# Values loaded by batch, ten weight units beside the packing, and products of another form, in a fused attention and expert kernel

## The chip, the cores and the metric

The kernel runs on one core of a Trainium2 chip. The metric is the device time of one execution in microseconds, the median of several runs, against the kernel before. The core has TensorE (PE, the matrix engine), VectorE (DVE), ScalarE (ACT), GpSimd (POOL) and SyncE (SP, which only issues transfers here), each with its own queue of instructions, taken in order. An instruction waits at the head of its queue until what it reads has been written and what it overwrites is free, and everything behind it waits too.

## The reference

Three parts follow each other. A packed attention with 8 batches (B), 8 heads (H), 576 positions (S), 64 dimensions a head and 32 pack rows: the pack rows attend to the keys and values, then every query attends to the packed rows. Its output, 4608 tokens of 512 values, goes through a feed-forward layer with 2048 hidden values, and the result through a layer with 8 experts, of which each token takes the one with the largest gate value.

```python
p_packed = sm_attn(p, k, v)                 # 32 packed rows per head
x = sm_attn(q, p_packed, p_packed)          # then [4608, 512]
h = x @ w_in                                # 512 -> 2048
g = np.where(h >= 1, h, np.where(h <= -1, 0.0, (h + 1) ** 2 / 4))
x = g @ w_out                               # 2048 -> 512
e = argmax(x @ w_gate)                      # one of 8 experts per token
out = softmax(x @ w_gate)[e] * (np.maximum(x @ w1[e], 0) @ w2[e])
```

## The kernel before

**Numbers in two parts.** Weights and activations of the large products are split into a high and a low part of a narrower type (F32R). A product of two such numbers is three matmuls: high by high, high by low, low by high.

**The packing** (function packing, loop over i from 0 to 17, NG = 16 iterations with work). Iteration i is one half of the heads of one batch. It has these steps: the keys are loaded into one of three buffers kp (L371), the values into one of three buffers vr (L379, L380; rows of 256 floats, 1 KB); PE makes the scores sc (L388); DVE takes the largest of each row, nm (L395), and scales it (L396); ACT takes the exponent (L398), with the sums rs, which DVE inverts (L399, L400); PE transposes the exponents in tp and av (L406, L408); ACT copies them into tA and tB, which lie behind the values in the buffer vr (L409 to L411); one iteration later PE multiplies them with the values (av, L421), and ACT scales the result into packed (L422).

**Weight units.** The first feed-forward layer has its weights in 16 units (FC) of 1 MB, as 64-bit numbers. Unit u is loaded by load_unit (L275) into a raw buffer of the list RAW and split by prep_unit: ACT Abs (L290), DVE L291 to L294 on 1024 elements a partition, ACT cast (L295), DVE subtraction (L296). Of four units the first two are input weights (ws), the other two output weights (wo). NU = 12 units are prepared in the packing, evenly over its 16 iterations, each two loads ahead; units 12 to 15 are prepared by late_unit in steps 3 to 6 of the first tile.

**Products.** The second attention is folded into the first layer: for a pair of batches p and each n from 0 to 3, the packed rows pk are multiplied with the input weights ws into pw (buffers pw0n and pw1n). For the first pair, first_product makes them from the units in place: for (n, g) and each of two halves par, 6 matmuls of 128x512 (L323), one cast on ACT (L326) and one subtraction on DVE (L327), each on 128 partitions. n = 0 and 1 are made in the packing loop, n = 2 and 3 behind it. The input weights are also spilled to memory (L299), and for later pairs reloaded and multiplied by product: for (n, k) 3 matmuls (L336), whose result is evacuated in two halves of 64 partitions (L340, L341).

**Steps.** Tile t of 12, step fc of 16: ffn1 makes h (L714: the product weights pw with the second attention's probabilities ah and al, which tile_chains makes in pieces from the queries, qr at L212), hidden makes the activation in rt (ACT L731 and L732, DVE L733) and its parts gh (ACT L747) and gl (DVE L748), two buffers of each of the three; tile_y of the step before adds into four rows of y (L719, L720, L721). The first LEAD = 3 steps are issued in the last iterations of the packing loop. The expert part begins when all tiles are done, and the change doesn't touch it.

**What sets the order.** Only SP's queue is in the order of the code. The instructions of the other engines are ordered by the framework's scheduler, by its own estimate of when each can run. Buffers are taken by tag: a tile of a tag with two buffers waits until the reader of the one before the last is done.

## Time and profile before

| | |
|---|---|
| median of 3 runs | 1271.33 us (1271.19 to 1272.02) |
| the profiled execution | 1273.13 us, its span 1271.4 us |
| mean granted TensorE clock in it | 0.981 |
| PE busy | 1205.7 us, 95% of the span |
| DVE busy | 943.2 us, 74% |
| ACT busy | 752.5 us, 59% |
| POOL busy | 420.8 us, 33% |
| moved by DMA | 128.25 MB, mean 101 GB/s |

The shares are means over stages with different limits. The change lies in the first 170 us, and there a table by stretches tells more: for each stretch it has the busy time of every engine, the granted clock, the mean share of time in which the 16 DMA engines were busy (somewhat over 1 where their packets overlap) and what they moved. A timeline gives the start of each instruction, its duration, engine, line and operation, and in brackets how long the engine had been idle and what released it. The durations of neighbours overlap, as the engines are pipelined: what an instruction costs its engine in a full queue is the distance between two starts.

### The profile page before, as it was taken

The page shows a single profiled execution, that of the slowest core. Times are in us where ns is not written, and L with a number is a line of the kernel's source. Part 1 is how long each engine was busy: PE and PEld are TensorE (multiplying, and loading weights), DVE is VectorE, ACT ScalarE, POOL GpSimd, SP SyncE. Part 2 cuts the span into 40 slices and gives each one's busy share as a digit, 9 for nine tenths or more (in the row PEclk, how much of TensorE's full clock was granted, in tenths as well). Part 3 has the DMA queues.
Part 4 walks back from the last instruction along what each step waited for, and adds up shares of the span by engine and source line. Part 5 has one row for each costly group of instructions (what it writes and reads, how often), then busy time and mean ns, then how long its engine had stood idle before and what let it go on. Part 6 is the DMA issues. An engine that isn't in the chain of part 4 may idle for free. (4 is left out here: it accounts for less than half of the span.)

```text
span 1271.4 us, 21999 instructions
## 1 busy us (share of the span) xinstructions
PE 1205.7 (95%) x7234; PEld 999.5 (79%) x7234; DVE 943.2 (74%) x2360; ACT 752.5 (59%) x1702; POOL 420.8 (33%) x682
## 2 busy tenths in 40 slices
PE   5788999999999999999999998988999999999997
PEld 3446887788778887778888876876999999989996
DVE  7787858988877859968679598698566666666663
ACT  4656646667656566566565555643656566565653
POOL 3120116624731116731112266776312112121110
PEclk8988999999999999999999999999999999999999
DMA  9994870143111232112331105201611212112150
GB/s 341 374 337 146 314 203 22 44 164 133 55 35 48 93 108 76 59 34 67 110 102 37 36 17 174 44 1 58 195 39 42 59 34 67 34 42 59 34 175 21
DMA packets 70186, 128.25 MB, mean 101 GB/s; under 512 B 10281, under 2 KB 46633, under 8 KB 66864
## 3 DMA queue, kind: packets, MB, share of 16 engines
q1 hardware_dynamic: 56464, 97.33, 23.7%
q0 software_dynamic: 5840, 18.95, 3.9%
q10 hardware_dynamic: 7760, 10.49, 2.7%
q8 instruction: 60, 0.98, 0.3%
q14 instruction: 62, 0.51, 0.1%
HBM read 162.31 MB, written 31.77 MB: 153 GB/s over the span
## 5 line engine op out<-in xcount | busy, mean ns | idle before, releaser
L714 PE MATMUL h<-ah,pw 128*128 128x256 f32 (+1 forms) x1024 | 244.0, 302 | 11.3 <-DVE rt L733 10.8
L886 PEld LDWEIGHTS gh<-gx,sw 128*128 128x128 f32 x1728 | 230.4, 192 | 14.5
L522 DVE CUSTOM_DVE_ANT_0 jk<-yr,wgb 128x512 bf16<-128x512 f32 x288 | 232.8, 808 | 5.1 <-ACT yr L773 3.2
L886 PE MATMUL gh<-gx,sw 128*128 128x256 f32 x1728 | 234.0, 284 | 0.0
L719 PE MATMUL y<-wo,gh 128*128 128x512 f32 x576 | 230.4, 400 | 1.1 <-ACT kp L398 0.6
L720 PE MATMUL y<-wo,gh 128*128 128x512 f32 x576 | 227.8, 396 | 0.0
L870 DVE TENSOR_TENSOR sw<-raw,sw 128x512 fp32r<-128x512 f32 x264 | 169.4, 692 | 76.3 <-ACT sw L869 76.3
L714 PEld LDWEIGHTS h<-ah,pw 128*128 128x128 f32 x1024 | 176.7, 190 | 36.5 <-DVE rt L733 20.3
L869 ACT CAST sw<-raw 128x512 fp32r<-128x512 f32 x304 | 169.3, 617 | 60.7 <-PE gy L721 54.2
L721 PE MATMUL y<-wo,gl 128*128 128x512 f32 x576 | 191.8, 399 | 2.4 <-POOL gl L748 2.0
L731 ACT ACTIVATE rt<-h,half 128x320 f32<-128x320 f32 (+1 forms) x192 | 110.9, 580 | 111.1 <-PE h L714 74.9
L714 PE MATMUL h<-al,pw 128*128 128x256 f32 (+1 forms) x512 | 152.6, 298 | 0.3 <-POOL al L243 0.3
L747 ACT CAST gh<-rt 128x256 fp32r<-128x256 f32 (+2 forms) x256 | 100.6, 417 | 86.8 <-DVE rt L733 64.6
L733 DVE SCALAR_TENSOR_TENSOR rt<-h,rt 128x320 f32<-128x320 f32 (+1 forms) x192 | 105.4, 550 | 62.0 <-ACT rt L732 60.3
L721 PEld LDWEIGHTS y<-wo,gl 128*128 128x128 f32 x576 | 106.0, 188 | 30.8 <-POOL gl L748 5.4
L719 PEld LDWEIGHTS y<-wo,gh 128*128 128x128 f32 x576 | 108.6, 188 | 25.0 <-issue 2.1
L720 PEld LDWEIGHTS y<-wo,gh 128*128 128x128 f32 x576 | 108.9, 189 | 18.4
L854 POOL TENSOR_TENSOR gx<-xT,gx 128x1024 fp32r<-128x1024 f32 (+1 forms) x19 | 45.1, 2373 | 235.9 <-ACT gx L853 220.8
L719 PE MATMUL gy<-sw,ggh 128*128 128x512 f32 x288 | 114.5, 398 | 0.0
L720 PE MATMUL gy<-sw,ggh 128*128 128x512 f32 x288 | 114.4, 397 | 0.0
L890 ACT ACTIVATE ggh<-gh 128x256 fp32r<-128x256 f32 x144 | 54.9, 382 | 98.5 <-PE gh L886 94.2
L748 DVE TENSOR_TENSOR gl<-rt,gh 128x64 fp32r<-128x64 f32 (+1 forms) x192 | 92.9, 499 | 22.7 <-ACT gh L747 15.9
(222 smaller groups left out, 1859.7 us busy)
## 6 DMA issues: line engine op xcount, KB each, us to landing
raw<-in_w2cat SPq DMA_DIRECT2D x76, 1024.0 KB
ws<-wsd SPq DMA_DIRECT2D x48, 512.0 KB
wr<-in_wcat SPq DMA_DIRECT2D x16, 1024.0 KB
kp<-in_kT SPq DMA_DIRECT2D x16, 576.0 KB
xb<-xs SPq DMA_DIRECT2D x72, 128.0 KB
vr<-in_vv SPq DMA_DIRECT2D x16, 512.0 KB
wsd<-ws SPq DMA_DIRECT2D x8, 1024.0 KB
qr<-in_qT ACTq DMA_DIRECT2D x16, 320.0 KB
```

The costliest lines, as they stand in the source:

```text
L522: dve.tensor_tensor_reduce(out=junk, in0=rows[j][:, :DM], in1=wgb[0][:, e, :], scale=1.0, scalar=0.0, op0=ALU.mult, op1=ALU.add, accum_out ...
L714: pe.matmul(ps[:, col0:col0 + n], lhsT=w[:, g, part, c], rhs=x[:, g, col0:col0 + n], start=(n_mm == 0), stop=(n_mm == 5))
L719: pe.matmul(y, lhsT=gh, rhs=wh, start=first, stop=False)
L720: pe.matmul(y, lhsT=gh, rhs=wl, start=False, stop=False)
L721: pe.matmul(y, lhsT=gl, rhs=wh, start=False, stop=last)
L731: act.activation(v[:, :W], ps[:, :W], AF.Relu, bias=half, scale=0.5)
L733: dve.scalar_tensor_tensor(out=v[:, :W], in0=ps[:, :W], scalar=1.0, in1=v[:, :W], op0=ALU.max, op1=ALU.min)
L747: act.copy(hi, v[:, c0:c1])
L748: lo_eng.tensor_tensor(out=lo, in0=v[:, c0:c1], in1=f32(hi), op=ALU.subtract)
L869: act.copy(w[:, 0, :], r)
L870: lo_engine(sid, i, n).tensor_tensor(out=w[:, 1, :], in0=r, in1=f32(w[:, 0, :]), op=ALU.subtract)
L886: pe.matmul(ps[:, :SL], lhsT=first(sid, 4 * (fc // 4) + k, part)[:, c], rhs=rh[:, k, :], start=(n_mm == 0), stop=(n_mm == 3 * KD - 1))
```

## The change

The loads of the values: s1_load_v now takes a batch at a time. 512 of its 576 rows go into one buffer as four consecutive rows of 512 floats for each partition (8 KB in one piece), the other 64 into a work tile (named vq) of tag rt. To fit, the transposes of iteration i take every fourth column of the exponents. tA and tB become work tiles of the tags gh and gl, and the third buffer of the values, wo6, becomes a fourth buffer for raw units, which are loaded three ahead.

The units: 10 instead of 12 are spread over the 16 iterations, units 10 and 11 go with the two iterations behind (i = 16 and 17), units 12 to 15 stay late. The load of the last unit is issued one iteration later, and so are the loads of qr for the first tile.

The products: for n = 2 and 3, first_product uses product_of, the body of product with the weights in place.

```diff
...
-    RAW = ["wo4", "wo5", "wr"] * 4 + ["pw03", "pw13", "wo7", "wr"]
+    RAW = ["wo4", "wo5", "wr", "wo6"] * 2 + ["wo4", "wo5", "wr", "wo6", "pw03", "pw13", "wo7", "wr"]
...
         if g == 0:
             products(0, n)
+        if n > 1:
+            for q in range(2):
+                product_of(0, n, 2 * g + q, wstage[2 * n + g][:, q])
+            return
         for par in range(2):
...
         if k == 0:
             products(p, n)
+        product_of(p, n, k, ws1[0][:, k % 2])
+
+    def product_of(p, n, k, w):
         g, q = divmod(k, 2)
         ps = a_tile([P, 512], f"pp{p}_{n}_{k}")
         for i, (t, m) in enumerate(((0, 0), (0, 1), (1, 0))):
-            pe.matmul(ps, lhsT=both(k, t), rhs=ws1[0][:, q, m, :], start=(i == 0), stop=(i == 2))
+            pe.matmul(ps, lhsT=both(k, t), rhs=w[:, m, :], start=(i == 0), stop=(i == 2))
         for par in range(2):
...
-            def s1_load_v(i):
-                b, g = divmod(i, 2)
-                s = d[i]
-                va = wtile(("pw02", "pw12", "wo6")[i % 3], [P, 1280 + 640], F32, f"vr{i}")
-                s["vr"] = va[:, :1280].rearrange("p (c d) -> p c d", c=5)
-                s["tA"], s["tB"] = va[:, 1280:1280 + 384], va[:, 1280 + 384:]
-                sp.dma_start(s["vr"][:, :4, :], vv[b, :512, 256 * g:256 * g + 256].rearrange("(c p) d -> p c d", p=P))
-                sp.dma_start(s["vr"][:64, 4, :], vv[b, 512:, 256 * g:256 * g + 256])
+            vrs = {}
+
+            def s1_load_v(b):
+
+                vr = wtile(("pw02", "pw12")[b % 2], [P, 4, 512], F32, f"vr{b}")
+                rest = work.tile([P, 512], F32, name=f"vq{b}", tag="rt", bufs=2)
+                sp.dma_start(vr, vv[b, :512].rearrange("(p c) d -> p c d", c=4))
+                sp.dma_start(rest[:64], vv[b, 512:])
+                vrs[b] = vr, rest
...
-                    pe.transpose(ps[:, c * P:(c + 1) * P], s["a1"][:, c * P:(c + 1) * P], ident)
+                    pe.transpose(ps[:, c * P:(c + 1) * P], s["a1"][:, :4 * P].rearrange("p (j c) -> p c j", c=4)[:, c], ident)
...
+                s["tA"] = work.tile([P, 384], F32, name=f"tA{i}", tag="gh", bufs=2)
+                s["tB"] = work.tile([P, 256], F32, name=f"tB{i}", tag="gl", bufs=2)
...
             s1_load_v(0)
             s1_load(1)
             load_unit(1)
+            s1_load(2)
             s1_load_v(1)
-            s1_load(2)
             load_unit(2)
+            load_unit(3)
...
-                soon(3 + 2 * c, load)
+                soon(4 + 2 * c, load)
...
-                if i + 2 < NG:
-                    s1_load_v(i + 2)
-                for u in range(-(-NU * i // NG), min(-(-NU * (i + 1) // NG), NU)):
+                if 2 <= i < NG - 2 and i % 2 == 0:
+                    s1_load_v(i // 2 + 1)
+
+                us = range(-(-(NU - 2) * i // NG), -(-(NU - 2) * (i + 1) // NG)) if i < NG else (NU - 2 + i - NG,)
+                for u in us:
                     prep_unit(u)
-                    if 0 < u < NU - 2:
-                        load_unit(u + 2)
+                    if 0 < u < NU - 3:
+                        load_unit(u + 3)
...
                 if i == NG - 1:
-                    for u in range(NU, FC):
+                    for u in range(NU, FC - 1):
                         load_unit(u)
+                if i == NG:
+                    load_unit(FC - 1)
...
```

From L318 on the lines move down by some: the score is now L396, nm L403 and L404, the value product L432, h L730, y L735 to L737, rt L749, gh L763 and gl L764, and the halves of a product L347 (ACT) and L348 (DVE).

Where instructions moved, the orders of the two programs show it. PE's queue at the end of the packing, of before; sc_1186 and sc_1238 are the scores of iterations 14 and 15, av_1166 the value product of 13, y_2 the first row of y, tp_1219 the transposes of 14:

```order
L388 MATMUL sc_1186<-kp_164 64x288 x4
L719 MATMUL y_2_1362<-wo_356,gh_1306 128x512
L720 MATMUL y_2_1362<-wo_356,gh_1306 128x512
L421 MATMUL av_1166<-vr_1059 32x64 x20
L388 MATMUL sc_1238<-kp_160 64x288 x4
L721 MATMUL y_2_1362<-wo_356,gl_1307 128x512
L714 MATMUL h_2_1383<-ah_193,pw_0_0_592 128x256
...
L406 MATMUL tp_1219<-ident,kp_164 128x128 x4
```

And of after, from the last transpose of iteration 14 (av_1218); av_1276 is the value product of 15, pp_2_0 the first product of n = 2:

```order
L416 MATMUL av_1218<-ident,kp_164 64x128
L396 MATMUL sc_1234<-kp_160 64x288 x4
L730 MATMUL h_1_1346<-ah_197,pw_0_0_585 128x256
...
L432 MATMUL av_1218<-vr_1117,tA_1220 32x64 x12
L432 MATMUL av_1218<-vr_1117,tB_1221 32x64 x4
L432 MATMUL av_1218<-vq_1118,tB_1221 32x64 x4
L416 MATMUL av_1276<-ident,kp_160 64x128
L414 MATMUL tp_1271<-ident,kp_160 128x128 x4
L432 MATMUL av_1276<-vr_1117,tA_1278 32x64 x12
...
L343 MATMUL pp_2_0_1440<-ws_1121,pk 128x512 x3
L735 MATMUL y_0_1367<-wo_424,gh_1302 128x512
```

Before, y of step 0 is begun ahead of the score of 15; now the first y stands behind the last value product and the first product.

DVE's queue around the last two nm, of before; ca_1178 is unit 10, rt_1308 and rt_1354 are the hidden steps 0 and 1:

```order
L733 SCALAR_TENSOR_TENSOR rt_1308<-h_0_1293,rt_1308 128x512
...
L294 SCALAR_TENSOR_TENSOR ca_1178<-wr_1001,ca_1178 128x1024
L733 SCALAR_TENSOR_TENSOR rt_1354<-h_1_1339,rt_1354 128x512
L395 TENSOR_REDUCE nm_1191<-sc_1186 128x1
L296 TENSOR_TENSOR wo_1177<-ca_1178,wo_1177 128x2x512
L396 TENSOR_SCALAR nm_1191<-nm_1191 128x1
L748 TENSOR_TENSOR gl_1353<-rt_1354,gh_1352 128x512
L395 TENSOR_REDUCE nm_1243<-sc_1238 128x1
L399 TENSOR_SCALAR rs_1194<-rs_1194 128x1
```

And of after, where ca_1336 is unit 10 and nm_1239 the nm of iteration 15:

```order
L291 TENSOR_SCALAR ca_1336<-ca_1336 128x1024
L292 TENSOR_SCALAR ca_1336<-ca_1336 128x1024
L293 SCALAR_TENSOR_TENSOR ca_1336<-wr_1061,ca_1336 128x1024
L749 SCALAR_TENSOR_TENSOR rt_1304<-h_0_1289,rt_1304 128x512
L403 TENSOR_REDUCE nm_1239<-sc_1234 128x1
L294 SCALAR_TENSOR_TENSOR ca_1336<-wr_1061,ca_1336 128x1024
L404 TENSOR_SCALAR nm_1239<-nm_1239 128x1
L296 TENSOR_TENSOR wo_1335<-ca_1336,wo_1335 128x2x512
...
L764 TENSOR_TENSOR gl_1303<-rt_1304,gh_1302 128x512
```

Before, hidden steps 0 and 1 (gl_1353 closes one of them) lie among the last nm, and unit 10 is finished ahead of the last; now only the first part of hidden step 0 does, and the end of unit 10 and gl of step 0 lie behind.

DVE's queue in steps 3 to 7, of before; ca_1625 is unit 14:

```order
L291 TENSOR_SCALAR ca_1625<-ca_1625 128x1024
L748 TENSOR_TENSOR gl_1647<-rt_1648,gh_1646 128x512
L292 TENSOR_SCALAR ca_1625<-ca_1625 128x1024
L327 TENSOR_TENSOR pw_2_1_1423<-pp_2_1_1_1452,pw_2_1_1423 128x512
L293 SCALAR_TENSOR_TENSOR ca_1625<-wr_1289,ca_1625 128x1024
L296 TENSOR_TENSOR ws_1561<-ca_1562,ws_1561 128x2x512
L327 TENSOR_TENSOR pw_3_0_1504<-pp_3_0_0_1506,pw_3_0_1504 128x512
L294 SCALAR_TENSOR_TENSOR ca_1625<-wr_1289,ca_1625 128x1024
L733 SCALAR_TENSOR_TENSOR rt_1690<-h_7_1675,rt_1690 128x512
```

And of after, where ca_1508 and ca_1572 are units 12 and 13:

```order
L294 SCALAR_TENSOR_TENSOR ca_1508<-wr_1283,ca_1508 128x1024
L234 TENSOR_SCALAR sm_0_0_1433<-sm_0_0_1433 128x10
L292 TENSOR_SCALAR ca_1572<-ca_1572 128x1024
L749 SCALAR_TENSOR_TENSOR rt_1489<-h_3_1474,rt_1489 128x512
L348 TENSOR_TENSOR pw_2_1_1439<-pp_2_2_1457,pw_2_1_1439 64x512
L348 TENSOR_TENSOR pw_2_0_1438<-pp_2_3_1465,pw_2_0_1438 64x512
L235 RECIPROCAL sm_0_0_1433<-sm_0_0_1433 128x10
L293 SCALAR_TENSOR_TENSOR ca_1572<-wr_1285,ca_1572 128x1024
L296 TENSOR_TENSOR ws_1507<-ca_1508,ws_1507 128x2x512
L764 TENSOR_TENSOR gl_1488<-rt_1489,gh_1487 128x512
L348 TENSOR_TENSOR pw_2_1_1439<-pp_2_3_1465,pw_2_1_1439 64x512
```

One subtraction of 128x512 between two operations of a unit became two of 64x512, and the hidden steps stand further apart in operations.

## Rows read from the trace of the kernel before

**Rows 1.** Stretches: length, busy PE, PEld, DVE, ACT, POOL, clock, DMA share, GB/s

```profile
0.00:110.00 110.00, 78.45 (x815) 45.71 (x815) 86.17 (x169) 64.97 (x159) 26.37 (x110) 0.84 0.98 346
113.60:159.70 46.10, 45.54 (x317) 37.59 (x316) 36.62 (x56) 29.74 (x50) 3.44 (x3) 1.00 0.59 223
140.00:150.00 10.00, 10.00 (x57) 8.62 (x57) 9.47 (x16) 7.62 (x12) 2.97 (x3) 1.00 0.69 288
150.00:160.00 10.00, 10.00 (x55) 8.54 (x54) 10.00 (x13) 6.72 (x10) 0.00 (x0) 1.00 0.83 302
170.00:180.00 10.00, 10.00 (x56) 8.45 (x55) 6.40 (x12) 6.98 (x13) 2.68 (x4) 1.00 0.99 353
```

**Rows 2.** PE's timeline: start, duration (us), engine, line, operation, out<-in, shape, count

```profile
117.09 0.39 PE L719 MATMUL y<-wo,gh 128*128 128x512 f32 x1
...
117.56 0.40 PE L721 MATMUL y<-wo,gl 128*128 128x512 f32 x1
...
121.64 0.39 PE L714 MATMUL h<-ah,pw 128*128 128x256 f32 x1
...
123.17 0.39 PE L719 MATMUL y<-wo,gh 128*128 128x512 f32 x1
...
125.73 0.60 PE L406 MATMUL tp<-ident,kp 128*128 128x128 f32 x4
...
129.80 0.90 PE L421 MATMUL av<-vr 128*32 128x64 f32 x40
130.63 1.66 PE L323 MATMUL pp<-ws,pk 128*128 128x512 f32 x6
...
164.46 0.39 PE L719 MATMUL y<-wo,gh 128*128 128x512 f32 x1
```

**Rows 3.** ACT's timeline, same columns, idle time before in brackets

```profile
115.41 0.74 ACT L398 ACTIVATE kp<-sc,nm 128x576 f32<-128x576 f32 x1
...
116.80 0.64 ACT L732 ACTIVATE rt<-rt 128x512 f32<-128x512 f32 x1
...
119.47 1.05 ACT L295 CAST wo<-ca 128x1024 fp32r<-128x1024 f32 x1 [0.38 <-DVE ca L294]
...
161.89 0.62 ACT L747 CAST gh<-rt 128x512 fp32r<-128x512 f32 x1
```

**Rows 4.** DVE's timeline, same columns

```profile
113.56 0.75 DVE L395 TENSOR_REDUCE nm<-sc 128x1 f32<-128x576 f32 x1
...
152.07 0.68 DVE L327 TENSOR_TENSOR pw<-pp,pw 128x512 fp32r<-128x512 f32 x1
152.68 1.21 DVE L294 SCALAR_TENSOR_TENSOR ca<-wr,ca 128x1024 int32<-128x1024 int32 x1
153.81 0.68 DVE L733 SCALAR_TENSOR_TENSOR rt<-h,rt 128x512 f32<-128x512 f32 x1
...
159.68 0.68 DVE L733 SCALAR_TENSOR_TENSOR rt<-h,rt 128x512 f32<-128x512 f32 x1
...
169.04 0.47 DVE L226 TENSOR_REDUCE mx<-qr 128x10 f32<-128x320 f32 x1
```

**Rows 5.** Line L341: duration min/median/max in ns; who waited for it

```profile
L341 DVE TENSOR_TENSOR pw<-pp,pw x96: 645/686/696, 246.3 to 684.6; 64x512 fp32r<-64x512 f32 x96
...
  ACT pw L340: 18.4, 23
```

**Rows 6.** Waits, 0 to 110 us: us in total, times, longest

```profile
SPq L212 <- POOL al L243: 10.4, 1, 10.4
...
PE tp L406 <- ACT kp L398: 11.8, 6, 3.1
...
DVE ca L291 <- ACT ca L290: 6.0, 7, 1.3
```

**Rows 7.** Stretches with a mix of loads, and with 8 KB pieces alone

```profile
12.00:62.00 50.00, 38.17 (x432) 21.44 (x430) 42.09 (x87) 32.74 (x95) 6.45 (x19) 0.90 1.05 375
130.00:136.00 6.00, 6.00 (x70) 4.47 (x60) 4.25 (x7) 4.53 (x7) 0.00 (x0) 1.00 1.02 427
```

More of the change, by code (lines that the diff above doesn't have):

```diff
@@ L415, in s1_av @@
                 ps = s["ps"][:, :D]
+                vr, rest = vrs[i // 2]
                 for c in range(5):
@@ L420, in s1_av @@
                         r = slice(NP * j, NP * j + NP)
-                        pe.matmul(ps[r, :], lhsT=t[:, r], rhs=s["vr"][:w, c, D * j:D * j + D], start=(c == 0), stop=(c == 4))
+                        pe.matmul(ps[r, :], lhsT=t[:, r], rhs=(vr[:, c] if c < 4 else rest[:w])[:, 256 * (i % 2) + D * j:256 * (i % 2) + D * j + D], start=(c == 0), stop=(c == 4))
                 act.activation(packed[:, i, :], ps, AF.Copy, scale=s["rs"])
```

## Prediction

> **What bounds the kernel now.** I read the table of stretches first [rows 1]. In the first 110 us no engine is full: PE is busy 78.45 us, VectorE (DVE) 86.17, and the DMA engines stand at a share of 0.98. Behind that PE is the bound: 45.54 of the 46.1 us from 113.6 on, and 10.00 of 10 in the stretches that follow. So the end of the kernel moves with two things: PE work that disappears where PE is full, and the moment from which PE is fed without gaps. The packing (score, softmax, transposes and value products of iterations 0 to 15) ends late there: the last nm is taken at 113.56, the last av runs at 129.80, and the first product of the late kind (L323) at 130.63, with steps of tile 0 woven in between [rows 2, 4]. While PE is full, DVE has 46.1 - 36.62 = 9.5 us of slack between 113.6 and 159.7, but none from 150 to 160 [rows 1]. That is where this change can go either way.
>
> The profiled execution took 1273.13 us (its span 1271.4), 1.8 above the median of 1271.33. My sum is a shift against the trace of that execution, and I add it to the median.
>
> **Fewer products.** The products n=2 and n=3 take 3 matmuls of 128x512 for each of 8 k instead of 6 for each of 8 halves: 24 fewer. Two starts of such matmuls that have one between them are 0.47 us apart (117.09, 117.56) [rows 2], 0.235 each. All of them lie behind 130 us, where PE is full: 24 x 0.235 = **5.6 us less on PE**.
>
> **What that costs elsewhere.** Each such result is now evacuated in two halves of 64 partitions: 16 casts on ACT and 16 subtractions on DVE instead of 8 and 8. The later pairs already do this: 64x512 takes 686 ns [rows 5], and the 128x512 form at 152.07 took 0.68 us [rows 4]. Half the partitions are no cheaper, so 8 more are a real load. Back to back a 512-element operation holds DVE for 0.61 us (152.07 to 152.68) and a 1024-element operation of a weight unit for 1.13 (152.68 to 153.81) [rows 4].
>
> **The shared buffers.** tA, tB and the rest of V now lie in the buffers of gh, gl and rt, two of each. The order of PE shows the effect: before, y of step 0 begins ahead of sc15; now the first y stands behind av15 and a product. Up to 130.63 the kernel before had done 44 matmuls of y (10.3 us at 0.235) and the steps h_2 to h_4, each 12 matmuls of 256 columns in 1.4 to 1.5 us (121.64 to 123.17), 4.4 us [rows 2]. So 14.7 us of PE work are pushed behind av15. If PE ran without a gap from av15 on, the change would come out even with av15 ending at 130.6 - 14.7 + 5.6 = **121.5**.
>
> When does av15 end? By the order, DVE has up to nm15 two gl and one rt less (3 x 0.61), L294 and L296 of one unit less (2 x 1.13), and one pair of rs more (0.3): 3.8 us less. With idle time as before, nm15 comes at 113.56 - 3.8 = 109.8. From there: nm (0.75), the L294 that now stands behind it, and L404, together 1.9; exp and the three copies, one after the other as at 115.41 to 116.80, 1.4; the transposes 0.6; av 0.9 [rows 2, 3]. That is 4.8 if ACT is free; with the Abs and the cast of a unit ahead of these steps (1.05 as at 119.47, twice) and 0.5 for hand-overs 7.4. I take 7.4: av15 ends at 117.2. By PE alone the change would gain 121.5 - 117.2 = **4.3 us**.
>
> **Two units moved behind.** Ten units are spread over the 16 iterations, the next two go into the two iterations behind them, four stay late. I count DVE's queue up to the hidden step of h_8 (before: L733 at 159.68 [rows 4]), since by then nearly all of it is done. After has, up to there, 9 more subtractions of products (9 x 0.61 = 5.5 us), L294 and L296 of the last unit (2.3), and 3 transposes, 4 reductions and two small ones of tile chains, 0.47 or less each (as at 169.04; 3.1): **10.9 us more**. Its slack was 9.5. With a long queue DVE was idle 0.53 us in 140 to 150 and 0.00 in 150 to 160 [rows 1]; at the first rate 46 us keep 2.4, at the second none. I take 2.0, so 7.5 of slack are used and L749 of h_8 starts at 159.7 + 10.9 - 7.5 = 163.1.
>
> When must it? The y of step 8 began at 164.46 [rows 2]. After has one score of a tile chain more ahead of it (estimate 0.3, two matmuls), and like before no product behind it: the even point is 164.8. From the start of L733 to the end of its gh cast it takes 1.3 us if nothing stands ahead (0.68 and 0.62), and it took 2.83 at 159.68 to 162.51 [rows 3, 4]. With 2.0 the even point for L749 is 162.8. So DVE and not PE decides: 163.1 is 0.3 late, and **the 4.3 us that PE had gained are waited away** in steps 1 to 8. Behind them DVE is light (6.40 of 10 in 170 to 180 [rows 1]), but PE is full and gives nothing back.
>
> **Values in 8 KB pieces.** 16 loads of 512 KB and 16 small ones become 8 of 1 MB and 8 small. Nobody on the path waits for them: DVE's largest wait in the first 110 us is L291 for ACT, 6.0 us, PE's behind the start is the transpose for exp, 11.8 [rows 6]. The start may lose: kp1 stands behind 0.6 MB more of V, 1.6 us at 375 GB/s [rows 7], covered by unit 0 on DVE; uncovered it costs 1.6. SP's stall of 10.4 us at qr, behind which loads of kp, V and units queue [rows 6], becomes shorter, since qr is loaded one iteration later. No wait of the path names a load there, so I take 0; if waits for raw units hide in it, up to 1 us is gained.
>
> The stretch with 8 KB pieces of raw units moved 427 GB/s, the mix of sizes 375 [rows 7]. 9.4 MB of V would take 22.0 instead of 25.1 us in the queue, 3.1 less, which stays covered. The Trainium skill ("DMA: Bandwidth & Descriptors", section Specifications) gives 512 B as the least transfer for the line rate. By that, 1 KB pieces would be there already, and the gain in the queue would be 0 instead of 3.1; the trace leaves this open, since the two stretches differ in rows and directions too.
>
> **The sum.** -5.6 (products), +1.3 (av15 at 117.2, where the pushed work alone would be even at 115.9), +4.6 (waits of PE for DVE up to step 8): +0.3. Forecast 1271.33 + 0.3 = **1271.6 us**: within the 0.2%, 2.5 us, that a measurement of this kernel can tell from no change.
>
> **Rivals.** A, faster: DVE keeps up. Its idle time in the first 110 us (110 - 86.17 = 23.8 [rows 1]) shrinks by 4, because one more raw unit is in flight and SP stalls less. Then L749 of h_8 comes at 159 and PE alone decides: -4.3, **1267.0**; with 4.8 from nm15 to av15, -6.9, 1264.4. For it speaks that L291 waits 6.0 us in there; against it that it waits for ACT's work in line, and not for loads [rows 6].
>
> B, slower: DVE, ACT and PE wait for one another in turn. L749 of h_1 can write rt only when av15 is done; L348 waits for its ACT half; behind both, in the same queue, stand the next L749 and L764, on which y hangs. If DVE keeps 5 us idle instead of 2 and the cast lags 2.8, L749 of h_8 starts at 166.1 against 162.0: +4.1, **1275.4**. It decides from about 4 us of DVE idle time between nm15 and h_8. For it: in the later pairs L341 waited 18.4 us for its ACT half in 23 places [rows 5]. Against it: from 150 to 160 a like mix ran without a gap [rows 1].
>
> C, the steady loads and the earlier packing do nothing: av15 ends at 121 as DVE's idle time grows by what its work shrinks, PE is even by itself, and the units moved fit beside it: **1271**, no change.
>
> **Chances.** Forecast and C, within 0.2%: 0.40. B and what lies beyond it: 0.32. A: 0.28. The range reaches into both: down to 1266.5 (A with little more), up to 1277.0 (B with the uncovered 1.6 of the start).
>
> **What would show it.** The last av ends at 115 to 119, with no y before it. Then PE has gaps of 4 to 5 us in all up to 165, which end with rt, gl or gh (L749, L764, L763), DVE is busy 9.5 or more of each 10 us from 110 to 160, and L749 of h_8 starts near 163. A would show PE at 10.00 from 120 on; B gaps of 8 and more, with DVE waiting for L347. I am wrong from the root if av15 ends behind 121, or if nm15 comes at another time than 107 to 112: then the packing itself runs at another pace than DVE's work count says.

## The result, and the profile after

| | before | after |
|---|---|---|
| median of 5 runs beside one another | 1271.55 us (1271.19 to 1273.73) | 1279.62 us (1278.91 to 1284.42) |
| profiled execution (its span) | 1273.13 (1271.4) | 1278.91 (1277.1) |
| ratio of the two kernels | | 1.0069, 95% interval 1.0051 to 1.0087 |

Slower by 0.7%. The prediction, 1271.6 with a range up to 1277.0, was wrong. The profiled executions differ by 5.8 us, the medians by 8.1: before's execution lay 1.6 above its median, and after's was the fastest of its five. The traces can explain 5.8.

First a mark that shows where the loss arises. The first copy of tile 0's result on ACT stands behind all of the woven part. Before and after (start, duration, engine, line, operation, out<-in, shape, count, idle time before and its releaser):

```profile
196.25 0.59 ACT L773 COPY yr<-y 128x512 f32<-128x512 f32 x1 [0.76 <-PE y L721]
```

```profile
201.53 0.59 ACT L789 COPY yr<-y 128x512 f32<-128x512 f32 x1 [0.77 <-PE y L737]
```

5.3 us late, and tiles 1 to 10 keep 5.0 to 5.3. So nearly all of it is made before the end of tile 0. The stretches of after, in the columns of [rows 1]:

```profile
0.00:110.00 110.00, 76.43 (x857) 45.22 (x858) 84.95 (x172) 64.16 (x162) 30.29 (x110) 0.86 0.95 346
113.60:159.70 46.10, 39.10 (x232) 30.07 (x232) 45.01 (x64) 31.59 (x50) 4.37 (x3) 0.95 0.77 268
140.00:150.00 10.00, 7.38 (x40) 5.81 (x40) 9.84 (x14) 7.34 (x11) 1.00 (x1) 1.00 0.62 234
150.00:160.00 10.00, 7.31 (x33) 5.33 (x32) 9.72 (x14) 4.03 (x6) 0.00 (x0) 0.77 1.10 297
154.00:156.00 2.00, 0.00 (x0) 0.00 (x0) 1.97 (x3) 0.08 (x1) 0.00 (x0) 0.85 1.02 254
156.00:158.00 2.00, 1.89 (x7) 0.95 (x8) 1.97 (x4) 0.62 (x1) 0.00 (x0) 0.50 1.06 352
```

In the 46.1 us where PE was busy 45.54 and DVE 36.62 [rows 1], PE is now busy 39.10 and DVE 45.01: they have changed places. In 154 to 156 PE does nothing at all, and in the 2 us behind that its granted clock is 0.50, the 1.2 GHz level. The row of 120 to 170 sums it up, before and after:

```profile
120.00:170.00 50.00, 50.00 (x343) 40.56 (x342) 38.62 (x57) 29.34 (x47) 4.52 (x5) 1.00 0.77 257
```

```profile
120.00:170.00 50.00, 43.81 (x219) 34.12 (x218) 46.26 (x69) 32.60 (x51) 7.86 (x8) 0.93 0.83 286
```

6.2 us of idle PE, and a clock below the full one. Over stretches of 5 us, busy time times the missing clock comes to 2.9. From 170 on PE is full at 1.00 up to the mark, as it was before. PE's waits from 110 to 172 in after (who waited, for what: us in total, times, longest):

```profile
PE h L730 <- DVE rt L749: 3.3, 3, 1.7
PE s L222 <- issue: 2.7, 1, 2.7
PE av L416 <- ACT kp L406: 1.1, 1, 1.1
PE y L737 <- DVE gl L764: 0.9, 1, 0.9
PE pp L343 <- DVE pw L348: 0.9, 1, 0.9
```

The 1.7 of the first row ended at 109.76 and the wait of the third at 113.36, both before the last av. Of the 6.2 from 120 on, 1.6 are for rt, 2.7 are the score's, 0.9 are for gl and 0.9 for pw.

Its timeline shows the largest hole, from 153.42 (152.26 + 1.16) to 156.11; and DVE's queue in the same stretch:

```profile
152.26 1.16 PE L737 MATMUL y<-wo,gl 128*128 128x512 f32 x4
156.11 1.34 PE L222 MATMUL s<-qr,pkf 128*64 128x320 f32 x4 [2.69 <-issue]
```

```profile
152.20 0.69 DVE L348 TENSOR_TENSOR pw<-pp,pw 64x512 fp32r<-64x512 f32 x1
152.92 1.22 DVE L293 SCALAR_TENSOR_TENSOR ca<-wr,ca 128x1024 int32<-128x1024 int32 x1
154.07 1.22 DVE L296 TENSOR_TENSOR wo<-ca,wo 128x1024 fp32r<-128x1024 f32 x1
155.31 0.69 DVE L348 TENSOR_TENSOR pw<-pp,pw 64x512 fp32r<-64x512 f32 x1
156.04 0.69 DVE L749 SCALAR_TENSOR_TENSOR rt<-h,rt 128x512 f32<-128x512 f32 x1
...
168.36 0.68 DVE L749 SCALAR_TENSOR_TENSOR rt<-h,rt 128x512 f32<-128x512 f32 x1
```

The score L222 waits for "issue", that is for nothing that the profile names. Its data qr had landed by 144. PE starts 0.11 us after the second L348 ends (156.00), and that L348 is the last reader of a product's PSUM bank; a score and a product share a set of banks. I infer that it waited for this bank. The same pair of times comes back wherever a score waits like this: with P alone (below), with halves alone and in the two kernels with the late units apart, PE starts 0.10 or 0.11 us after such a subtraction ends. With P alone:

```profile
163.01 0.69 DVE L348 TENSOR_TENSOR pw<-pp,pw 64x512 fp32r<-64x512 f32 x1
163.80 1.33 PE L222 MATMUL s<-qr,pkf 128*64 128x320 f32 x4 [3.81 <-issue]
```

In after, the subtraction stood in DVE's queue behind two operations of a weight unit, 1.22 us each, and L749, on which the next h hangs, behind both. The last row is L749 of h_8.

In the first 110 us SP's stall of 10.4 us at qr [rows 6] has shrunk to 1.9. SP now waits longest at the loads of V, for the av that frees their buffer (us in total, times, longest):

```profile
SPq L386 <- PE av L432: 22.9, 4, 10.1
```

### The profile page after: what moved, and what is told of

The parts are those of the page before. It is cut to its first block, busy times and chain, and to the rows that moved or that the text cites. A ratio compares the mean times of both kernels' runs of the same rounds, so it can differ in the third digit from the quotient of the medians.

```text
span 1277.1 us, 21947 instructions
## 1 busy us (share of the span) xinstructions
PE 1202.7 (94%) x7210; PEld 997.8 (78%) x7210; DVE 949.6 (74%) x2368; ACT 756.1 (59%) x1710; POOL 426.7 (33%) x682
## 5 line engine op out<-in xcount | busy, mean ns | idle before, releaser
L730 PE MATMUL h<-ah,pw 128*128 128x256 f32 (+1 forms) x1024 | 244.9, 304 | 14.7 <-DVE rt L749 14.1
L735 PE MATMUL y<-wo,gh 128*128 128x512 f32 x576 | 231.2, 402 | 0.7 <-ACT gh L763 0.7
L730 PEld LDWEIGHTS h<-ah,pw 128*128 128x128 f32 x1024 | 177.1, 191 | 41.4 <-DVE rt L749 25.1
L737 PE MATMUL y<-wo,gl 128*128 128x512 f32 x576 | 190.2, 400 | 3.2 <-POOL gl L764 1.9
L730 PE MATMUL h<-al,pw 128*128 128x256 f32 (+1 forms) x512 | 153.1, 299 | 0.7 <-POOL al L243 0.7
L763 ACT CAST gh<-rt 128x256 fp32r<-128x256 f32 (+2 forms) x256 | 100.7, 417 | 88.9 <-DVE rt L749 66.2
L749 DVE SCALAR_TENSOR_TENSOR rt<-h,rt 128x320 f32<-128x320 f32 (+1 forms) x192 | 105.4, 550 | 60.8 <-ACT rt L748 58.3
L737 PEld LDWEIGHTS y<-wo,gl 128*128 128x128 f32 x576 | 105.8, 189 | 33.0 <-POOL gl L764 5.3
L735 PEld LDWEIGHTS y<-wo,gh 128*128 128x128 f32 x576 | 109.1, 189 | 23.9 <-ACT gh L763 2.0
L735 PE MATMUL gy<-sw,ggh 128*128 128x512 f32 x288 | 114.1, 396 | 0.0
L764 DVE TENSOR_TENSOR gl<-rt,gh 128x64 fp32r<-128x64 f32 (+1 forms) x192 | 91.6, 492 | 22.2 <-ACT gh L763 15.1
```

The lines of the kernel that those rows point to most:

```text
L730: pe.matmul(ps[:, col0:col0 + n], lhsT=w[:, g, part, c], rhs=x[:, g, col0:col0 + n], start=(n_mm == 0), stop=(n_mm == 5))
L735: pe.matmul(y, lhsT=gh, rhs=wh, start=first, stop=False)
L737: pe.matmul(y, lhsT=gl, rhs=wh, start=False, stop=last)
L749: dve.scalar_tensor_tensor(out=v[:, :W], in0=ps[:, :W], scalar=1.0, in1=v[:, :W], op0=ALU.max, op1=ALU.min)
L763: act.copy(hi, v[:, c0:c1])
L764: lo_eng.tensor_tensor(out=lo, in0=v[:, c0:c1], in1=f32(hi), op=ALU.subtract)
```

## The experiments

Three parts are to be told apart: V (values by batch, with tA, tB and the rest of V in the buffers of gh, gl and rt, a fourth raw buffer with loads three ahead, and the later qr), U (ten units spread, two behind) and P (the products n=2 and n=3 in the half form). Times are medians, with the ratio against the kernel before in the same runs; before measured 1272.3 to 1273.5 there, so two kernels are compared by their ratios. The lag is that of tile 0's first copy against 196.25 in the profiled execution. It comes from one execution, which lies up to 4.3 us off the median of its kernel, so it belongs to the holes in the same trace and only roughly to the median. My theory by now was rival B: DVE's queue is too full, and PE, DVE and ACT wait in turn. Against it stood the shared buffers, the loads, and something of the new product form itself.

**One part put back, or DVE relieved.** Three kernels made from after. Only the products put back to the old form:

```
-        if n > 1:
+        if n > 3:
```

> The changed kernel with the products of n=2 and n=3 in the old form (6 matmuls, 128 partitions). Theory: PE gets 5.6 us more, DVE 4.9 less; as PE waits for DVE in the changed kernel, the extra matmuls go into its gaps: 1275 to 1279, the same or some us faster than the changed kernel. Rival (PE's work decides, the gaps are of another origin): 1284 to 1286.

Measured: 1276.8, ratio 1.0025 (1.0013 to 1.0037). PE is at 50.00 of 50 from 120 on, so all the holes there are the work of P; but the last av ends at 119.1, not at 116, and the lag is still 4.8. This profiled execution was the slowest of eight (1280.24), and its clock fell to 0.50 from 119 to 121, so the lag is high for this kernel. By the ratios (1.0069 and 1.0025) P costs 5.6 us within after, and 3.2 stay.

All twelve units spread over the packing again:

```
-                us = range(-(-(NU - 2) * i // NG), -(-(NU - 2) * (i + 1) // NG)) if i < NG else (NU - 2 + i - NG,)
-                for u in us:
+                for u in range(-(-NU * i // NG), min(-(-NU * (i + 1) // NG), NU)):
```

> The changed kernel with twelve units spread over the 16 iterations of the packing, as before, nothing late but units 12 to 15. Theory: two units (10 us of DVE work) leave the stretch behind nm15 and go ahead of it; nm15 comes some 4 us later (the slack was in front of it only in part), the gaps of PE up to 165 shrink by more: 1273 to 1277. Rival (the shared buffers): 1279 to 1284, since av15 ends later and the pushed steps with it.

Measured: 1281.14, 1.0060 (1.0048 to 1.0073), lag 3.8. This is the rival's range, and not the theory's. The last av ends at 118.3, and PE still waits 4.4 us for rt from 110 to 172: with fewer late units the holes stay.

The gl of tile 0 on POOL instead of DVE:

```
-        lo_eng = pool if tile_kind(t) == "A" else dve
+        lo_eng = pool if tile_kind(t) == "A" or t == 0 else dve
```

> The changed kernel, with the subtraction gl of the first tile's 16 steps on POOL instead of DVE; nothing else. Theory (DVE's queue from 110 to 165 us is what PE waits for): 16 x 0.61 = 9.8 us leave DVE, the gaps of PE between 116 and 165 (6.2 us in the changed kernel, and the stretch at half clock behind the last of them) mostly vanish, and the time falls by 5 to 9 us, to 1271 to 1275. Rival (the tile steps pushed behind av15 by the shared buffers rt, gh and gl are the loss, whoever subtracts): 1278 to 1281, no change; POOL takes 1.5 us instead of 0.69 for such a subtraction, so it could even lose.

Measured: 1278.08, 1.0034 (1.0023 to 1.0046), lag 3.6. DVE is relieved by 2.4 us in 113.6 to 159.7 (42.59 instead of 45.01), and 1.7 of the lag go; by the ratios about half of the loss goes (1.0034 against 1.0069), less than the theory's 5 to 9 us. PE's holes from 120 to 170 shrink to 4.0 us, and that of the score is gone, but the clock falls earlier, to 0.50 from 115 to 121.

**Each part alone**, on top of the kernel before. P:

```
+        if n > 1:
+            for q in range(2):
+                product_of(0, n, 2 * g + q, wstage[2 * n + g][:, q])
+            return
...
```

> The kernel before, with the products n=2 and n=3 of the first pair in the new form, nothing else. Theory: PE loses 5.6 us of work, DVE gets 8 x 0.61 = 4.9 us more in a stretch where it has 9.5 us of slack, so most of the 5.6 comes out: 1266 to 1268. Rival (halves of 64 partitions cost DVE and ACT what PE saves): 1270 to 1273.

Measured: 1280.2, 1.0057 (1.0043 to 1.0071), lag 4.9. Both ranges on record, 1266 to 1268 and 1270 to 1273, were missed: the part that takes 5.6 us from PE makes the kernel slower all by itself. The waits of PE from 110 to 172, and the stretch with the largest:

```profile
PE s L222 <- issue: 3.8, 1, 3.8
PE h L721 <- DVE rt L740: 1.8, 1, 1.8
```

```profile
120.00:170.00 50.00, 42.77 (x246) 34.42 (x246) 39.75 (x55) 30.74 (x48) 5.57 (x4) 0.90 0.69 242
160.00:170.00 10.00, 6.20 (x23) 4.83 (x24) 8.72 (x13) 5.76 (x10) 1.49 (x1) 0.66 1.08 290
```

It is the picture of after: an h that waits for rt (until 145.06, behind it a clock of 0.58 in 145 to 147), and a score that waits for no named thing (until 163.80, behind it 0.50). DVE's busy time from 120 to 170 hardly grew (39.75 against 38.62). So the sum of DVE's work is not what broke.

U, with three raw buffers as before:

> The kernel before with ten units spread over the 16 iterations and two in the two behind, nothing else. Theory: the packing ends earlier by the work of up to two units, but 10 us of DVE work move into the slack of 9.5 us behind: before within 2 us. Rival (DVE overload makes PE wait): before plus 4 or more.

Measured: 1274.39, 1.0016 (1.0008 to 1.0025), lag 0.0. Two more late units alone cost 1.8, none of it up to the end of tile 0.

V, that is after with the old products and twelve units:

> The changed kernel with the old products and with twelve units in the packing: what is left is the values by batch, the shared buffers, four raw units three ahead and the later qr loads. Theory: the 14.7 us of pushed tile work need av15 at 116 or before to come out even, and DVE's work up to nm15 is as before less 1.8 us for the hidden steps: av15 at 117 to 120, before plus 2 to 5 us, 1275 to 1278. Rival (steadier loads speed up the packing): before or faster, 1268 to 1273.

Measured: 1278.14, 1.0040 (1.0027 to 1.0053), lag 4.9. PE is full from 120 on, and the last av ends behind 120.58 + 0.32:

```profile
120.58 0.32 PE L432 MATMUL av<-vq,tB 64*32 64x64 f32 x8
```

The prediction put the even point for this, without the products, at 115.9. 120.9 is 5.0 behind it, and the lag is 4.9. The parts don't add up: 6.7 (P), 1.8 (U) and 5.5 (V) alone, 8.1 together.

**V taken apart.** The loads alone, with tA, tB and the rest of V in buffers of their own:

```
-                va = wtile(("pw02", "pw12", "wo6")[i % 3], [P, 1280 + 640], F32, f"vr{i}")
...
+                vr = wtile(("pw02", "pw12")[b % 2], [P, 4, 512], F32, f"vr{b}")
+                sp.dma_start(vr, vv[b, :512].rearrange("(p c) d -> p c d", c=4))
...
+                s["tA"], s["tB"] = tt[:, h:h + 384], tt[:, h + 384:h + 640]
...
```

> The kernel before with the values loaded by batch in 8 KB pieces, but with tA, tB and the rest of V in the buffer wo6 instead of those of gh, gl and rt (raw units then keep three buffers); units and products as before. Theory (the shared buffers made the loss of 5.5 us of the values alone, by pushing tile steps behind av15): before plus or minus 2. Rival (the loads themselves, their order or the strided transposes cost it): before plus 3 to 6.

Measured: 1272.29, 1.0001 (0.9992 to 1.0010), lag -0.8. The larger pieces cost nothing and bring nothing. The Trainium skill ("DMA: Bandwidth & Descriptors", section Specifications) gives 512 B as the least transfer for the line rate, by which 1 KB pieces are already large enough. This run goes with it, but doesn't prove it, as the queue was not what the kernel waited for.

The sharing of tA and tB alone, with the old loads:

```
...
+                s["tA"] = work.tile([P, 384], F32, name=f"tA{i}", tag="gh", bufs=2)
+                s["tB"] = work.tile([P, 256], F32, name=f"tB{i}", tag="gl", bufs=2)
```

> The kernel before with nothing changed but tA and tB, which are work tiles of the tags gh and gl, as in the changed kernel; values in halves of a batch as before. Theory: y of step 0 and the steps behind it wait for the value products of 14 and 15, av15 ends at 118 to 121 against an even point of 115.9, before plus 2 to 5. Rival: before plus or minus 1.

Measured: 1275.37, 1.0025 (1.0015 to 1.0035), lag 0.9. The last av ends at 116.6, earlier than the 118 to 121 expected and 0.7 behind the even point 115.9:

```profile
116.06 0.54 PE L422 MATMUL av<-vr,tB 128*32 128x64 f32 x16
```

So the larger loads by themselves cost nothing, and the sharing of tA and tB by itself costs 0.9 of V's 4.9 at the mark (2.9 of 5.5 by medians). The rest comes with what neither of the two kernels has: the rest of V in rt, the fourth raw buffer with loads three ahead, the later qr, or all of it together. Which of them is not shown. With V alone the loss at the mark is that of the moment at which the last av ends; with the sharing alone that moment explains 0.7, and PE also stood idle for 1.4 us from 127.41 on.

**P taken apart.** The old six matmuls, but each result evacuated in two halves of 64 partitions:

```
-            act.copy(o[:, g, 0, :], ps)
-            dve.tensor_tensor(out=o[:, g, 1, :], in0=ps, in1=f32(o[:, g, 0, :]), op=ALU.subtract)
+            for r in (slice(0, P),) if n < 2 else (slice(0, D), slice(D, P)):
+                act.copy(o[r, g, 0, :], ps[r, :])
+                dve.tensor_tensor(out=o[r, g, 1, :], in0=ps[r, :], in1=f32(o[r, g, 0, :]), op=ALU.subtract)
```

> The kernel before with its own products (6 matmuls), whose results for n=2 and n=3 are evacuated in halves of 64 partitions: 8 casts and 8 subtractions more, no matmul less. Theory: the added operations alone make the loss, before plus 4 to 8 us, 1276 to 1281. Rival (DVE's slack of 9.5 us behind 113 us takes the 4.9 us more): before plus 0 to 1.

The new three matmuls, evacuated over 128 partitions at once:

```
...
+        if p == 0:
+            o = wprod[n][q]
+            act.copy(o[:, g, 0, :], ps)
+            dve.tensor_tensor(out=o[:, g, 1, :], in0=ps, in1=f32(o[:, g, 0, :]), op=ALU.subtract)
+            return
```

> The kernel before with the three-matmul products for n=2 and n=3, each evacuated by one cast and one subtraction of 128 partitions instead of two of 64 each; the halves then lie in the wrong places, so the products n=2 and n=3 of the first pair are not the reference's. As many evacuations as before, 24 matmuls fewer. Theory (it is the 8 casts and 8 subtractions more, in a full DVE queue, that hold the PSUM banks and stop PE): the 5.6 us of PE come out, 1266 to 1269 where before stands at 1271.5 to 1273.5. Rival (the short products themselves, with their other place in the order, cost it): 1276 to 1280, as with the halves.

Halves alone: 1280.18, 1.0063 (1.0048 to 1.0079), lag 6.0. Three matmuls with whole evacuations: 1265.54, 0.994 (0.9926 to 0.9953), lag -2.4; this kernel leaves out the sorting of the halves, so its products, and with them its expert work, are not those of the reference, and only the lag counts. The two rows of 120 to 170, halves first:

```profile
120.00:170.00 50.00, 46.20 (x308) 36.79 (x301) 40.96 (x56) 31.22 (x50) 4.93 (x4) 0.93 0.67 241
```

```profile
120.00:170.00 50.00, 46.73 (x316) 36.92 (x305) 38.82 (x58) 30.87 (x51) 6.45 (x6) 1.00 0.84 274
```

The halves cost 6.0 us on the old matmuls and 7.3 (4.9 + 2.4) on the new ones. Between P alone and the whole evacuations idle PE time is 7.2 against 3.3, and the clock loses 4.1 us against none. So in these executions about half of the price is waiting, and half the clock behind the waiting.

P for n=3 alone and for n=2 alone:

```
+        if n == 3:
...
```

> The kernel before with the new form for n=3 alone: 12 matmuls fewer (2.8 us of PE), 4 casts and 4 subtractions more. If the slack of DVE decides (9.5 us, of which 4 halves take 2.4), the gain comes out: before minus 3 to before minus 1. If each half costs the same wherever DVE is busy (12 us for 8 in the run of products alone), half of its loss: before plus 2 to 5.

```
+        if n == 2:
...
```

> The same for n=2 alone, whose halves come first, from 130 us on, where DVE has been idle just before. If the slack decides: before minus 3 to before minus 1. If each half costs the same: before plus 2 to 5.

n=3: 1272.91, 1.0009 (1.0000 to 1.0018), lag -1.2. n=2: 1278.53, 1.0046 (1.0032 to 1.0059), lag 3.9. By medians n=3 (+0.6) lies between its two ranges and n=2 (+6.2) beyond both. Both add the same four casts and four subtractions and save 2.8 us of PE; so four pairs of halves cost 1.6 in the one place and 6.7 in the other. The place of n=2 lies earlier. PE's and DVE's timelines there:

```profile
146.63 0.39 PE L721 MATMUL h<-ah,pw 128*128 128x256 f32 x1 [1.80 <-DVE rt L740]
```

```profile
142.89 1.30 DVE L348 TENSOR_TENSOR pw<-pp,pw 64x512 fp32r<-64x512 f32 x2
144.23 1.23 DVE L294 SCALAR_TENSOR_TENSOR ca<-wr,ca 128x1024 int32<-128x1024 int32 x1
145.37 0.48 DVE L233 TENSOR_REDUCE sm<-qr 128x10 f32<-128x320 f32 x1
145.88 0.69 DVE L740 SCALAR_TENSOR_TENSOR rt<-h,rt 128x512 f32<-128x512 f32 x1
```

rt stands behind two halves, an operation of a unit and a reduction, and DVE is busy 9.87 of the 10 us from 140 to 150. But the place of n=3 is as full, with 9.91 of 10 from 150 to 160, and the longest hole there is 0.74 us, with the clock at 1.00:

```profile
150.00:160.00 10.00, 8.54 (x42) 6.44 (x41) 9.91 (x13) 6.75 (x11) 0.00 (x0) 1.00 0.93 338
```

So a full DVE alone doesn't set the price. What else does, the order of the single operations or the state of the banks, these two runs don't show.

**The late units spread out.** If what counts is what stands in the queue at one time, the late units should be moved apart. First their steps alone (3, 5, 7, 9 instead of 3 to 6), with P and with all of after:

```
-        at(LEAD + u - NU, lambda u=u: late_unit(u))
...
+        at(LEAD + 2 * (u - NU), lambda u=u: late_unit(u))
...
```

> The kernel before with the new products (as in the run of products alone, before plus 6.7 us), and with the late units 12 to 15 prepared in steps 3, 5, 7 and 9 instead of 3 to 6. Theory (the halves cost so much because they stand in a DVE queue that is full from 130 to 165 us): 20 us of DVE work are spread over twice the time, the banks come free earlier, PE keeps most of the 5.6 us: before minus 5 to before minus 1. Rival (four evacuations for three matmuls hold a bank too long in any queue): still before plus 4 to 7.

> The changed kernel with the late units in steps 3, 5, 7 and 9. Theory: the same relief; av15 ended at 116 us there, 5.5 before the even point of 121.5, and this comes out as far as PE's gaps go: before minus 4 to before plus 2. Rival (waits of single halves, whatever else is queued): before plus 5 to 8, as the changed kernel.

Measured: 1279.32, 1.0057 (1.0043 to 1.0071) and 1281.18, 1.0068 (1.0054 to 1.0082). They tell nothing on the question: DVE's queue stood in the same order (with P operation for operation from 106 to 185 us), since the scheduler, as I take it, places a unit where its data is there. The first is thus a second look at P alone. The same hole for rt of 1.79 us now left the clock at 1.00, and the lag is 3.7 instead of 4.9. To change the order, the data must come later: the loads of the last two units in steps 6 and 9.

```
...
+    for u, l, m in ((12, 0, 3), (13, 0, 4), (14, 6, 8), (15, 9, 11)):
+        if l:
+            at(l, lambda u=u: load_unit(u))
+        at(m, lambda u=u: late_unit(u))
...
```

With P, with P and gl of tile 0 on POOL, with all of after, and with neither, as a control:

> The kernel before with the new products, and with the raw loads of units 14 and 15 issued in steps 6 and 9 and the units prepared in steps 8 and 11. Spacing late_unit alone had left DVE's order as it was, since the scheduler takes a unit when its data is there; now two units (10 us of DVE work) stand behind the last halves in the order. Theory (the halves cost what they cost because DVE is full from 130 to 165 us): of the 6.7 us of loss most goes, before minus 3 to before plus 2. Rival (four evacuations of a bank are slow in any queue): before plus 5 to 7.

> As the new products with units 14 and 15 later, and with gl of the first tile on POOL besides: 20 us of DVE work out of the stretch in all. Theory: PE's waits are gone but for single ones, the 5.6 us of the matmuls come out: before minus 6 to before minus 2. Rival: before plus 3 to 6.

> The changed kernel with units 14 and 15 loaded and prepared later in the same way. Theory: 10 us of DVE work leave the stretch from 116 to 160, the time falls from before plus 8 to before plus 0 to 3. Rival: before plus 6 to 9.

> The kernel before with its own products, and units 14 and 15 loaded and prepared later. Theory: nothing waits for DVE there, so nothing is gained: before plus or minus 1. Rival (DVE's queue costs the kernel before something too): before minus 2 or less.

Measured:

| | median | ratio (95%) | lag |
|---|---|---|---|
| P | 1280.4 | 1.0069 (1.0056 to 1.0082) | 2.7 |
| P, gl on POOL | 1276.46 | 1.0038 (1.0026 to 1.0050) | 1.1 |
| after | 1278.66 | 1.0060 (1.0047 to 1.0073) | 2.4 |
| control | 1277.35 | 1.0047 (1.0034 to 1.0060) | -1.1 |

By their own expectations all three kernels with P fell to the rivals or beyond them, and the control missed its plus or minus 1: it loses 5.0 us. None of that lies before the end of tile 0; its mark turns to 1.0 to 2.8 late in tiles 2 to 5. From 195 to 385 us PE is busy 184.86 of 190 there instead of 187.51, with waits for rt, gl and gh; why these come late is open. Against the control P costs 3.8 at the mark instead of 4.9 and 3.0 instead of 6.7 by medians; with gl on POOL (for which there is no control of its own) it costs 2.2 at the mark and gains 0.9 by medians. So, measured against the control, a shorter queue takes back a part of the price at the mark. It doesn't take back all: with gl on POOL, DVE is busy only 36.42 of 50 us, less than before, and PE still stands idle 5.5. The mean hides that DVE is as full as ever where the holes lie, from 135 to 145:

```profile
120.00:170.00 50.00, 44.51 (x269) 35.50 (x269) 36.42 (x51) 32.63 (x52) 14.14 (x11) 0.97 0.69 238
135.00:145.00 10.00, 6.76 (x35) 4.90 (x33) 9.85 (x14) 6.17 (x10) 2.35 (x2) 1.00 0.40 165
```

No version that computes the reference beat the kernel before.

## Why the prediction was wrong

**The packing: right.** nm15 was forecast at 109.8, the last av to end at 117.2, no y ahead of it. After:

```profile
109.62 0.75 DVE L403 TENSOR_REDUCE nm<-sc 128x1 f32<-128x576 f32 x1
```

```profile
115.72 0.32 PE L432 MATMUL av<-vq,tB 64*32 64x64 f32 x8
115.96 0.96 PE L343 MATMUL pp<-ws,pk 128*128 128x512 f32 x3
116.76 0.40 PE L735 MATMUL y<-wo,gh 128*128 128x512 f32 x1
```

116.0 and 116.76. That nm15 came right to 0.2 us is partly luck: up to it DVE had 5.2 us less work than before (84.57 against 89.73), where I had counted 3.8, and stood idle 1.2 longer (25.05 against 23.83), where I had put no change. By PE alone the kernel would have been 5.5 us ahead of the even point 121.5.

**The 14.7 us pushed behind av15: right.** The even point worked out from them held where PE is full behind av15 at a clock of 1.00: with V alone the av15 of the same trace gives 5.0, and 4.9 are measured. With the sharing alone it gives 0.7 and 0.9 are measured, but there PE stood idle 1.4 us besides, so this agreement is partly luck. With the old products and ten units av15 ends at 119.1, 3.2 behind 115.9, and the clock lost up to 1.3 more between 110 and 170; the lag was 4.8.

**The loads: right.** I took 0 for them, with up to 1.6 at the start; the loads in buffers of their own measured 1.0001.

**DVE and not PE decides: right for the waits, wrong for h_8.** PE's waits behind av15 are for DVE, that of the score by inference. L749 of h_8 had to come at 162.8 to be even; it came at 168.36, 5.6 late, and the profiled time is 5.8 longer. But this is no test of the even point. PE's last hole ends at 156.11, and behind it PE ran without one up to the mark. DVE and ACT were waiting by then, ACT for PE and DVE for ACT:

```profile
160.34 0.69 ACT L747 ACTIVATE rt<-h,half 128x512 f32<-128x512 f32 x1 [2.96 <-PE h L730]
162.00 1.22 DVE L296 TENSOR_TENSOR wo<-ca,wo 128x1024 fp32r<-128x1024 f32 x1 [2.15 <-ACT wo L295]
```

So h_8 is late because PE already was, and not the other way round.

**The price of the halves: wrong, and this is the step that failed.** "Half the partitions are no cheaper, so 8 more are a real load" was right [rows 5], but I entered them in a sum: 10.9 us more work against 9.5 of slack less 2.0, 0.3 late. The sum says when a queue is done, not who stands in it. From nm15 to h_8 it took 58.7 us instead of the 53.3 forecast: 53.4 of work, 2.1 more than I counted, and 5.3 idle instead of 2.0:

```profile
109.62:168.36 58.74, 50.52 (x323) 39.05 (x324) 53.42 (x78) 38.61 (x63) 6.87 (x6) 0.94 0.76 260
```

In the sum this is the term +4.6, the waits of PE for DVE up to step 8. In its place the trace has 6.2 us of waits and 2.9 of lower clock, 9.1 in all. And PE didn't fall behind at the end of this queue. It fell behind in the middle, each time that an rt, a gl or the release of a bank stood behind halves and 1.2-us operations. P alone shows it best: its eight subtractions are 4.9 us at 0.61, DVE had 9.5 to spare, and by my sum it should have gained 5.6. It lost 4.9 at the mark. The halves cost 6.0 to 7.3 us there, 1.6 for n=3 alone and 6.7 for n=2 alone.

**The clock: missing.** I priced a hole by its length. In after the holes of 6.2 us cost 2.9 more by the clock; with P alone 7.2 cost 4.1. At av15 after was 5.5 ahead; 6.2 + 2.9 makes it 3.6 late, and 5.3 is measured, so 1.7 stay without a row. They stay as well with twelve units spread (av15 3.2 ahead, 5.2 idle, the clock at 1.00: 2.0 against 3.8). The same sum for the others (idle from 120 to 170, the clock's loss, less the saved matmuls, against the lag): P alone 7.2 + 4.1 - 5.6 = 5.7 against 4.9; halves 3.8 + 2.4 = 6.2 against 6.0; whole evacuations 3.3 - 5.6 = -2.3 against -2.4; n=3 alone 1.7 - 2.8 = -1.1 against -1.2; n=2 alone 3.3 + 1.3 - 2.8 = 1.8, with 0.7 of idle time behind 170 2.5, against 3.9.

**Rival B** was nearer than my forecast, and right in part. DVE stood idle 5.3 us between nm15 and h_8, about the 5 that it assumed, and an h waited for rt where it put that. But its sign, DVE waiting for L347, is not there: DVE's waits from 110 to 172 in after are 3.2 us at L296 for ACT L295, 1.5 at L241 for POOL and 0.5 at L291. Its price, 4.1, was too small: it knew neither the bank nor the clock. "From 150 to 160 a like mix ran without a gap" [rows 1] was the argument that misled: a stretch at 10.00 has no room left, and like it is not the same. PE's gaps, 6.2, lie between my 4 to 5 and its 8 and more; only with the clock's 2.9 do they reach its 8.

**Open:** how much of the halves' price is the full queue and how much the bank that two evacuations hold longer than one; that the bank is what L222 waits for is inferred, from an end and a start that lie 0.10 or 0.11 us apart in five kernels; why n=3 costs so much less than n=2; the 1.7 us without a row; which part of V, beside the sharing of tA and tB, makes its loss; and why the control's waits in the later tiles grow.

## What to carry to other kernels

Slack that is summed over a stretch doesn't cover anything by itself: take the order of the queue, and ask of each operation on which PE hangs what stands ahead of it, and for how long. An operation on half of the partitions cost as much here as on all (0.69 and 0.68 us on DVE, 0.58 and 0.59 on ACT), so a form that saves matmuls and doubles evacuations moves work from the engine that was the bound to the one that feeds it. And where several parts of a change act on one queue, read the loss at a mark in the program, part by part, as the whole times don't add up.

## What the runs showed of the hardware

A hole in a full stream of matmuls can cost more than its length. After the hole of 2.69 us the granted clock was 0.50, the 1.2 GHz level, in 156 to 160. With P alone 3.81 us of waiting were followed by 0.50 in 164 to 168, with halves alone 2.51 us by 0.50 in 164 to 168, and with n=2 alone 1.80 us by 0.50 in 148 to 150:

```profile
156.00:160.00 4.00, 3.89 (x16) 2.95 (x17) 3.82 (x7) 0.62 (x1) 0.00 (x0) 0.50 1.13 284
164.00:168.00 4.00, 4.00 (x17) 3.03 (x16) 3.97 (x7) 1.66 (x2) 0.07 (x1) 0.50 1.10 208
164.00:168.00 4.00, 2.94 (x14) 2.52 (x12) 3.94 (x6) 1.87 (x3) 0.68 (x1) 0.50 1.10 271
148.00:150.00 2.00, 2.00 (x9) 1.71 (x8) 1.97 (x6) 1.93 (x3) 0.76 (x1) 0.50 0.79 328
```

The length of the hole doesn't settle it. With P, the loads later and gl on POOL, a hole of 2.17 us that ended at 166.40 left the clock at 1.00. Two holes of 1.08 and 0.81 us before the last av left it at 1.00 in after, and the same two were followed by 0.50 in after with gl on POOL:

```profile
168.00:170.00 2.00, 2.00 (x11) 1.36 (x12) 2.00 (x2) 1.32 (x2) 2.00 (x1) 1.00 1.05 335
116.00:120.00 4.00, 4.00 (x22) 2.65 (x19) 4.00 (x6) 2.62 (x5) 0.00 (x0) 1.00 0.98 399
117.00:121.00 4.00, 4.00 (x11) 2.86 (x9) 3.42 (x4) 3.23 (x5) 0.00 (x0) 0.50 1.02 424
```

Before, 0.56 us of idle time between 110 and 120 left it at 1.00, and so did 3.3 us with whole evacuations, in holes of up to 0.9, and 5.2 us with twelve units spread, in holes of up to 1.5.
